# A fused state-space scan and squared-ReLU feed-forward: a new order for the front of the program

## The chip, the cores and the metric

One core of a Trainium2 chip runs the whole kernel. The metric is device time in microseconds, the median of several executions, lower being better. TensorE (PE in the profile, PEld for its weight loads), VectorE (DVE), ScalarE (ACT), GpSimd (POOL) and the DMA queues each work through a list of instructions of their own, in order, and wait for each other by semaphores. So the order in which the kernel records instructions decides what stands behind what on each engine.

## What is computed

Four batches of eight heads over 768 steps go through a chunked linear recurrence; its output, 3072 rows of 256, goes through a feed-forward layer with a squared ReLU. All inputs and the output are float32.

```python
for c in range(nc):                                   # chunks of 32 steps
    cum = np.cumsum(la, axis=-1)                      # la = log a
    L = np.exp(cum[..., :, None] - cum[..., None, :]) * causal
    M = np.einsum('bhin,bhjn->bhij', Cc, Bc) * L
    y_intra = np.einsum('bhij,bhjd->bhid', M, xc)
    y_inter = np.einsum('bhin,bhnd->bhid', Cc, state) * np.exp(cum)[..., None]
    y[:, :, sl] = y_intra + y_inter
    state = decay_full * state + np.sum(Bx, axis=2)   # Bx = B x decay_from_j
h = np.maximum(y_rows @ w_in, 0.0)                    # (3072,256) @ (256,2048)
out = h * h @ w_out                                   # (3072,2048) @ (2048,256)
```

## The kernel before

**Units and blocks.** The rows are cut into twelve units of 256 steps, one batch each: units 0 to 3 are the first third of the steps for the four batches, 4 to 7 the second, 8 to 11 the last. A unit's result, T, is one block of 256 rows of the feed-forward part; the blocks are called a to l.

**A unit, step by step.** `pc`, `pb` and `px` scale C, cast B and scale x by the running products of the decay, C and B into the tile jt, x into xs. `tr` transposes jt on TensorE (for the first four units) and `tc` copies the result out of PSUM into bct, in halves. `mt` computes the scores into PSUM banks 0 to 3, one bank for each quarter. Each quarter is multiplied by the causal mask: by VectorE straight out of PSUM (`mk`), or by a copy on ScalarE (`sc`) and then a product on VectorE or GpSimd (`ms`). `u` computes the state sums, `in` (or its halves `ina` and `inb`) applies the masked scores to the values, and `ca` adds what the earlier state carries in. `t` copies the two PSUM halves of the block into T (the letters behind the colon name the engine of each half), `us` copies the state sums. `sf` makes the state for the second half of a first-third unit (the tile Sd) directly from PSUM, `za`/`zb` and `sa`/`sb` the later ones.

**A block.** Up-projection `a0` to `a7`: four matmuls of 256 columns into one PSUM bank, two contraction halves for each of two output halves, then a ReLU on ScalarE (tile hb). `qa0` squares on VectorE (tile h). Down-projection `A0` to `A7`: four matmuls of 256 columns into an accumulator in bank 6 or 7. The same with the letters b to l. So T[a] and the w_in group are needed for an up-projection, a square and the w_out group for a down-projection.

**Decay products.** `sk` scans the first 256 steps, `sp` transforms the result on TensorE, `su` sums it, `to` and `ps` copy it out, `iv` takes inverses, `fq` spreads the totals into Pquad. `sn`, `p2` and `pq` are the same for the other 512 steps: `sn` ends with pick_p on VectorE, `p2` is eight transform matmuls and two of the totals.

**Loads.** The inputs of the units go through the SP queue (and a few through ACT's), in the order of the units. The weights, 2 MB each in float32, are cast on the way in by transfers that GpSimd issues (`wi0` to `wi3`, `wo0` to `wo3`, two up- or down-projections' worth each), so their place in GpSimd's own list of instructions sets when they start.

**Idle matmuls.** `id3:512` is three matmuls of ones with 512 columns whose result nobody reads, into a PSUM bank that is free.

**What sets the order.** `ORDER` is a text of such names, worked off from the first to the last by `one`; the tile framework adds the waits. A small bookkeeping (`turn`, `busy`, `bank`) hands out PSUM banks 0 to 5 in the order in which they were last used. From `rg4` on, the units 4 to 11 and the blocks c to l follow a regular rhythm.

Of the kernel before, what the change touches and what calls it, by code (L numbers as in the profile page):

```python
# [30 lines left out]
def kernel(  # L31
# [18 lines left out]
        ldx0:l:a wm jz0:v mb jz1:v ldB1:s id3:512 sk pbh0:a id2:512 pk pbl0:p wi0 sp pc0:v ldC1:s trB0 wi1 su iv1:0:8  # L50
        trC0 tcC0:0:v tcB0:2:a id1:512 tcC0:1:a ps pb1:a to px0:v jz2:v mt0 id1:512 u0:67 ldx1:s pc1:p fq sc0 mk0
        id1:512 mk0 ms0:p tr1 tc1:1:v sc0 tc1:0:a sf0 mt1 ldB2:s wo0 ldC2:s ms0:v ldx2:s id1:384 in0 ca0 iv:8:16
        id3:512 px1:p t0:aa id1:256 mk1 a0 a1 mk1 mk1 mk1 u1 ina1 inb1 sn1 us0 sf1 qa0 a3 ldC3:s wi2 fr p2 wi3 ca1
        qa1 wo1 pc2 pb2:a t1:vv us1 iv:32:64 a2 zb0 qa2 zb1 A0 ldB3:s wo2 ldx3:s b3 qb3 b0 pq b2 b1 tr2 wo3 sb1 qa3
        qb0 A1 b5 b4 qb1 qb2 qb5 tc2:1:v qb4 tc2:0:a a5 B0 b6 B1 a7 qa5 iv:16:32 px2 a6 mt2 B3 A2 sc2 u2 b7 us2 pb3:a
        pc3 mk2 qa6 px3 mk2 A5 ms2:v mk2 ld4 qb6 sf2 a4 qa7 B5 pc4 A6 A3 ld5 pb4 ina2 inb2 tr4 ca2 t2:aa tr3 B4 B2
        tc3:0:a tc3:1:a u3:45 qb7 ld6 ld7 mt3 qa4 B6 mk3 mk3 mk3 mk3 us3 c4 c5 c0 A4 A7 B7 c6 qc0 za3 qc4 c1 qc5 qc6
        sa3 px4 qc1 pc5 pb5 bk c2 rg4 tr5 C0 mk4 mk4 qc2 c7 qc7 sb0 c3 qc3 d2 d1 C5 za4 afC2 d0 C1 px5 C4 qd2 zb3 C6
        C3 qd0 d3 C2 mk4 mk4 C7 px6 sa4 rg5 qd3 sb3 pc6 zb4 sb4 pb6 D0 d4 qd1 tr6 mk5 za5 zb5 sa5 sb5 D1 iv:64:96 mk5
        d5 qd4 D2 pb7 d6 qd5 d7 qd6 D3 zb2 e0 qd7 mk5 e1 qe0 sb2 D4 mk5 D5 ld8 pc7 e2 qe1 D6 e3 qe2 px7 D7 rg6 e4 qe3  # L60
        za6 sa6 tr7 zb6 mk6 e5 qe4 sb6 e6 qe5 e7 qe6 mk6 E0 E1 E2 E3 ld9 px8 mk6 f0 qe7 E4 f1 qf0 pc8 E5 pb8 E6 mk6
        f2 qf1 f3 qf2 E7 rg7 mk7 F0 f4 qf3 za7 tr8 F1 F2 f5 qf4 f6 qf5 f7 qf6 g0 qf7 zb7 sa7 sb7 mk7 F3 mk7 F4 pc9
        pb9 px9 ld10 g1 qg0 F5 mk7 g2 qg1 F6 g3 qg2 F7 rg8 za8 zb8 sa8 sb8 g4 qg3 G0 mk8 tr9 g5 qg4 G1 mk8 g6 qg5 G2
        g7 qg6 G3 mk8 h0 qg7 G4 pc10 pb10 px10 ld11 h1 qh0 G5 mk8 h2 qh1 G6 h3 qh2 G7 rg9 za9 zb9 sa9 sb9 h4 qh3 H0
        mk9 tr10 h5 qh4 H1 mk9 h6 qh5 H2 h7 qh6 H3 mk9 i0 qh7 H4 pc11 pb11 px11 i1 qi0 H5 mk9 i2 qi1 H6 i3 qi2 H7
        rg10 za10 zb10 sa10 sb10 i4 qi3 I0 mk10 tr11 i5 qi4 I1 mk10 i6 qi5 I2 i7 qi6 I3 mk10 j0 qi7 I4 j1 qj0 I5 mk10
        j2 qj1 I6 j3 qj2 I7 rg11 za11 zb11 sa11 sb11 j4 qj3 J0 mk11 j5 qj4 J1 mk11 j6 qj5 J2 j7 qj6 J3 mk11 k0 qj7 J4
        k1 qk0 J5 mk11 k2 qk1 J6 k3 qk2 J7 rg12 k4 qk3 K0 k5 qk4 K1 k6 qk5 K2 k7 qk6 K3 l0 qk7 K4 l1 ql0 K5 l2 ql1 K6
        l3 ql2 K7 l4 ql3 L0 l5 ql4 L1 l6 ql5 L2 l7 ql6 L3 ql7"""
    WIN = [(0, 2), (2, 4), (4, 6), (6, 8)]  # L70
    WOUT = [(0, 2), (2, 4), (4, 6), (6, 8)]

# [154 lines left out]

    def ph_mask(k, q):
        nc.vector.tensor_tensor(out=live[k]["mts"][:, q].rearrange("p r g i -> p (r g i)"),  # L229
                                in0=pp[:, q, :], in1=mask, op=ALU.mult)  # L230
# [533 lines left out]
```

## Time and profile before

| | us |
|---|---|
| three runs of the kernel | 116.53, 116.64, 118.09 |
| their median | 116.64 |
| the profiled execution | 116.84 |
| its span, from the first instruction to the last | 115.1 |
| TensorE busy within the span | 108.9 (95%) |
| VectorE, ScalarE, GpSimd busy | 84.2, 76.7, 49.8 |

The granted clock of TensorE was 1.00 throughout. Times in a row of the timeline are the start from the beginning of the span and the length, both in microseconds; a row with x4 is four instructions merged, from the start of the first to the end of the last. What stands in square brackets is the engine's idle time just before the row, and what ended it. In the chain of waits a row is a stretch of time, with what the last instruction waited for at that point. TensorE's rows overlap by the depth of its pipeline, so that starts, not lengths, are compared. L numbers are lines of the kernel.

### The profile page before, as it was taken

How to read it: one execution, taken by the hardware profiler on the slowest of the kernel's cores; microseconds unless marked ns; L12 is line 12 of the kernel's file. 1: busy time of each engine (PE TensorE's matmuls, PEld its weight loads, DVE VectorE, ACT ScalarE, POOL GpSimd, SP SyncE). 2: the span in 40 equal slices, each digit the busy share in tenths (PEclk: the TensorE clock that was granted, in tenths of full speed). 3: DMA queues.
4: the chain of work that ended last, by engine and by line, in shares of the span. 5: the costliest groups of instructions: out<-in, count | busy, mean ns of one | idle time of the engine just before them, and what ended most of it. 6: DMA issues, size and time to landing. Idle time of an engine off the chain costs nothing.

```text
span 115.1 us, 3998 instructions
## 1 busy us (share of the span) xinstructions
PE 108.9 (95%) x1623; PEld 93.5 (81%) x1623; DVE 84.2 (73%) x187; ACT 76.7 (67%) x161; POOL 49.8 (43%) x102
## 2 busy tenths in 40 slices
PE   7977969999999999999999999999999999999990
PEld 2344749978898989989989989989989899899980
DVE  2469996779599969969965989849668488445530
ACT  0655667865598756787486686786777776876840
POOL 7369972068599457548602669038020020000000
PEclk9999999999999999999999999999999999999999
DMA  1999999989999913935915926623023020020202
GB/s 29 199 196 145 199 203 189 215 167 210 180 191 211 214 24 108 160 89 155 179 46 122 178 97 123 132 95 73 0 100 68 0 100 0 6 91 0 91 0 91
DMA packets 47814, 13.46 MB, mean 117 GB/s; under 512 B 44276, under 2 KB 45876, under 8 KB 47796
## 3 DMA queue, kind: packets, MB, share of 16 engines
q1 hardware_dynamic: 43828, 10.64, 44.8%
q0 software_dynamic: 1664, 2.10, 10.8%
q10 hardware_dynamic: 2304, 0.48, 2.0%
q8 instruction: 12, 0.20, 0.8%
q14 instruction: 6, 0.05, 0.1%
HBM read 10.58 MB, written 3.15 MB: 119 GB/s over the span
## 4 chain that ended last, share of the span: by engine, by line
PE 87%; DMA 6%; POOL 2%; issue 1%; DVE 1%; ACT 1%; ACTq 0%; DVEq 0%
PE pp L430 36%; PE pp L403 36%; PE pp L245 6%; DMA w_out_b<-in_moe_w_out_dram 6%; PE pp L476 4%; PE pp L220 3%; POOL mts L238 1%; PE pp L195 1%; POOL jt L158 1%; PE pp L452 1%; DVE jt L158 0%; DVE Sd L343 0%; ACT bct L208 0%; PE pp L521 0%; ACT osl L722 0%
## 5 line engine op out<-in xcount | busy, mean ns | idle before, releaser
L408 ACT ACTIVATE hb<-pp 128x512 bf16<-128x512 f32 x96 | 55.0, 599 | 24.7 <-PE pp L403 23.1
L430 PE MATMUL pp<-w_out_b,h 128*128 128x256 bf16 (+1 forms) x400 | 54.3, 268 | 0.8 <-DMA w_out_b<-in_moe_w_out_dram 0.8
L414 DVE TENSOR_TENSOR h<-hb 128x512 bf16<-128x512 bf16 x96 | 45.0, 486 | 12.7 <-ACT hb L408 12.3
L403 PE MATMUL pp<-T,w_in_b 128*128 128x256 bf16 x384 | 54.2, 273 | 0.0
L403 PEld LDWEIGHTS <-w_in_b 128*128 128x128 bf16 x384 | 41.4, 114 | 2.2 <-issue 1.0
L430 PEld LDWEIGHTS <-h 128*128 128x128 bf16 x400 | 37.6, 98 | 5.4 <-DVE T L210 1.1
L229 DVE TENSOR_TENSOR mts<-pp,mask 128x512 bf16<-128x512 f32 x45 | 29.6, 677 | 3.3 <-PE pp L220 3.3
L331 POOL TENSOR_TENSOR Sd<-z,Pquad 128x256 bf16<-128x256 f32 x16 | 11.1, 693 | 32.9 <-DVE z L315 25.7
L177 POOL TENSOR_TENSOR xs<-x_nat,Pinv 128x256 bf16<-128x256 f32 (+1 forms) x19 | 14.4, 776 | 5.2 <-DVE Pinv L546 4.6
L158 POOL TENSOR_TENSOR jt<-C_nat,P_sb 128x128 bf16<-128x128 f32 x22 | 9.4, 449 | 1.5 <-ACT P_sb L688 1.0
L476 PE MATMUL pp<-const-bfloat16-1.0 128*128 128x512 bf16 (+2 forms) x19 | 7.3, 516 | 0.8 <-PEq L748 0.8
L315 DVE SCALAR_TENSOR_TENSOR z<-z,Ptot,us 128x64 f32<-128x64 f32 x8 | 2.2, 281 | 6.3 <-ACT us L299 5.4
L437 ACT COPY osb<-pp 128x512 f32<-128x512 f32 x11 | 6.3, 584 | 0.4 <-PE pp L430 0.4
L245 PE MATMUL pp<-mts,xs 64*32 64x128 bf16 x384 | 5.9, 219 | 0.1
L170 POOL CAST jt<-B_nat 128x128 bf16<-128x128 f32 x17 | 5.4, 341 | 1.4 <-DMA B_nat<-in_B_dram 1.4
L220 PE MATMUL pp<-bct 32*64 32x256 bf16 x192 | 5.1, 279 | 0.9 <-DVE bct L210 0.6
L476 PEld LDWEIGHTS <-const-bfloat16-1.0 128*128 128x128 bf16 x19 | 2.2, 122 | 4.0 <-issue 3.7
L245 PEld LDWEIGHTS <-xs 64*32 64x32 bf16 x384 | 4.2, 90 | 0.6 <-issue 0.4
L282 ACT CAST T<-pp 128x512 bf16<-128x512 f32 x7 | 4.1, 592 | 0.4 <-PE pp L245 0.2
L208 ACT CAST T<-pp 128x256 bf16<-128x256 f32 x8 | 2.6, 375 | 2.6 <-PE pp L245 2.6
L245 PE MATMUL pp<-bct,Sd 128*128 128x128 bf16 x40 | 4.2, 220 | 0.0
L220 PEld LDWEIGHTS <-bct 32*64 32x64 bf16 x192 | 2.1, 102 | 2.0 <-issue 0.6
(62 smaller groups left out, 53.4 us busy)
## 6 DMA issues: line engine op xcount, KB each, us to landing
x_nat<-in_x_dram SPq DMA_DIRECT2D x11, 256.0 KB, 3.7
out_dram<-osb SPq DMA_DIRECT2D x11, 256.0 KB, 3.2
B_nat<-in_B_dram SPq DMA_DIRECT2D x11, 128.0 KB, 3.1
C_nat<-in_C_dram SPq DMA_DIRECT2D x11, 128.0 KB, 3.4
w_in_b<-in_moe_w_in_dram POOLq DMA_DIRECT2D x4, 256.0 KB, 6.8
w_out_b<-in_moe_w_out_dram POOLq DMA_DIRECT2D x4, 256.0 KB, 8.2
x_nat<-in_x_dram ACTq DMA_DIRECT2D x2, 128.0 KB, 3.4
bct<-jt SPq DMA_TRANSPOSE x8, 3.6
```

The source lines that it names most:

```text
L158: eng.tensor_tensor(out=_fap(jt[k % 3], 128 + 144 * g, [[384, 2], [32, 4], [1, 16]]), in0=_fap(loaded[k]["C"], 128 * g, [[16, 2], [32, 4], ...
L177: eng.tensor_tensor(out=_fap(xs, 256 * r, [[256, 2 // n], [32, 8], [1, 32]]), in0=_fap(loaded[k]["x"], 32 * r, [[32, 2 // n], [64, 8], [1, ...
L220: nc.tensor.matmul(pp[64 * u:64 * u + 64, q, r * 256:r * 256 + 256], bct[32 * q:32 * q + 32, r, 0, u * 64:u * 64 + 64], _fap(bct[32 * q:32 ...
L229: nc.vector.tensor_tensor(out=live[k]["mts"][:, q].rearrange("p r g i -> p (r g i)"), in0=pp[:, q, :], in1=mask, op=ALU.mult)
L245: nc.tensor.matmul(dst, w, v, start=bool(need), stop=False, skip_group_check=True, **({} if pos is None else {"tile_position": pos}))
L331: nc.gpsimd.tensor_tensor(out=_fap(S_d, 0, [[128, 2], [32, 4], [1, 32]]), in0=_fap(z, 0, [[32, 2], [0, 4], [1, 32]]), in1=_fap(Pquad, 4 * ...
L403: nc.tensor.matmul(pp[:, h, i * 256:(i + 1) * 256], _fap(w, g * w.shape[2] + (o // 2) * 512 + 2 * (o % 2) + i, [[4, 128]]), T[blk][:, g].r ...
L408: nc.scalar.activation(out=hb.rearrange("p i t -> p (i t)"), in_=pp[:, h, :], func=AF.Relu)
L414: nc.vector.tensor_tensor(out=h2, in0=hb, in1=hb, op=ALU.mult)
L430: nc.tensor.matmul(dst, h2[:, i, r * 128:(r + 1) * 128], w_out_b[gi][:, 2 * o + i, c0:c1], start=first, stop=(fp == 7 and i == 1), skip_gr ...
L437: nc.scalar.copy(out=osb, in_=pp[:, 6 if blk == 1 else 7, :])
L476: nc.tensor.matmul(pp[:, h, 0:int(cols)], ones_b[:, 0:128], ones_b[:, 0:int(cols)] if dep is None else dep, start=True, stop=True, skip_gr ...
```

## The change

The ORDER up to `rg4` is written anew, and from there on it is as before. The up-projection gets a form with a part, `a3:0` and `a3:1`, which issues the two matmuls of the first and then of the second contraction half; between the two the bank is held. `sf` gets a form on ScalarE (`sf2:a`), four activations that scale by a column of Pquad. Other new helpers (scores by halves, T by halves, named banks) are there but not called: `HALF` is empty, and no name with `@`, `tg` or `ca` with a part stands in the ORDER.

In the ORDER itself:

- Unit 0: one idle matmul of 256 columns is added ahead of `sp`. The inverses come ahead of C's product, the C transposes ahead of the totals `su`, and 1408 idle columns ahead of the C transposes. Three quarters are masked by VectorE out of PSUM and one by a copy and GpSimd, where it was two and two. Between `in0` and `ca0` stand 1024 idle columns; the 1792 behind `ca0` are gone.
- GpSimd: clearing jt2 (`jz2`) and the B casts of units 1 to 3 are GpSimd's now; they were VectorE's and ScalarE's. `wo0` stands ahead of `fq` and `ms0`.
- Copies: T0 is split between VectorE and ScalarE, T1 is ScalarE's; both copies of unit 1's transposes are ScalarE's.
- VectorE: `sf1` stands ahead of the second scan `sn`, and the scan behind unit 1's masks and the T0 copy; the products `px2` and `px4` are VectorE's (GpSimd's before).
- TensorE: a3, a2, b0, b2, b5, a7, a6 and b6 are up-projections in two parts. b0, b1 and half of b2 stand ahead of `A0`.
- Unit 2: its four quarters are masked by VectorE, `sf2` is ScalarE's. Unit 3: one quarter goes by ScalarE and GpSimd.

The core of the diff:

```diff
-        ldx0:l:a wm jz0:v mb jz1:v ldB1:s id3:512 sk pbh0:a id2:512 pk pbl0:p wi0 sp pc0:v ldC1:s trB0 wi1 su iv1:0:8
+        ldx0:l:a wm jz0:v mb jz1:v ldB1:s id3:512 sk pbh0:a id2:512 pk pbl0:p id1:256 sp trB0 id1:512 id1:384 iv1:0:8
...
-    def mm1(blk, fp):
-
-        h = bank()
+    opened = {}
+
+    def mm1(blk, fp, part=None):
+
+        h = opened.pop((blk, fp)) if part == 1 else bank()
         gi, o = group_of(WIN, fp)
         w = w_in_b[gi]
         for i in range(2):
-            for g in range(2):
+            for g in (0, 1) if part is None else (part,):
                 nc.tensor.matmul(pp[:, h, i * 256:(i + 1) * 256],
                                  _fap(w, g * w.shape[2] + (o // 2) * 512 + 2 * (o % 2) + i, [[4, 128]]),
                                  T[blk][:, g].rearrange("p r u t -> p (r u t)"),
-                                 start=(g == 0), stop=(g == 1), skip_group_check=True)
+                                 start=(g == 0 and (part is None or i == 0)), stop=(g == 1), skip_group_check=True)
+        if part == 0:
+            opened[(blk, fp)] = h
+            busy.add(h)
+            return
+        busy.discard(h)
...
-    def ph_sd_first(k):
+    def ph_sd_first(k, eng=None):
...
+        if eng is nc.scalar:
+            for q in range(4):
+                nc.scalar.activation(out=_fap(S_d, 32 * q, [[128, 2], [1, 32]]),
+                                     in_=_fap(pp, v["h"][0] * 512 + 256, [[32, 2], [1, 32]]),
+                                     func=AF.Copy, scale=Pquad[:, total(0, b, 0), q:q + 1])
+            v["S"] = [None, S_d]
+            return
```

On GpSimd, from the second w_in transfer on, there stood before (jt1 is unit 1's tile for B and C, sc0 a copied quarter of unit 0's scores and mts0 its masked scores):

```order
L139 DMA w_in_b1_113<-in_moe_w_in_dram 128x2x512
L158 TENSOR_TENSOR jt1_110<-C_nat1_179,P_sb_105 128x2x4x16 x2
L527 TENSOR_TENSOR Pquad_108<-Ptot_107,quad_93 128x32
L238 TENSOR_TENSOR mts0_218<-sc0_0_241,mask_90 128x512
L143 DMA w_out_b0_116<-in_moe_w_out_dram 128x1024
L177 TENSOR_TENSOR xs1_324<-x_nat1_236,Pinv_106 128x512
```

Unit 1's C product was the first thing behind the transfer. With the change, from the same transfer on:

```order
L142 DMA w_in_b1_113<-in_moe_w_in_dram 128x2x512
L749 MEMSET jt2_111 128x768
L173 CAST jt1_110<-B_nat1_159 128x2x4x16 x2
L161 TENSOR_TENSOR jt1_110<-C_nat1_193,P_sb_105 128x2x4x16 x2
L146 DMA w_out_b0_116<-in_moe_w_out_dram 128x1024
L572 TENSOR_TENSOR Pquad_108<-Ptot_107,quad_93 128x32
L257 TENSOR_TENSOR mts0_219<-sc0_2_232,mask_90 128x512
L180 TENSOR_TENSOR xs1_288<-x_nat1_222,Pinv_106 128x512
```

The clearing and two casts now stand ahead of the C product, and the first w_out transfer ahead of Pquad and the masked quarter.

On VectorE, around unit 1's masks and the second scan, there stood before (Sd is a state, a_cl, cp and pick_p the second scan, h a square):

```order
L343 TENSOR_TENSOR Sd0_0_258<-pp_120,Pquad_108 128x256
L238 TENSOR_TENSOR mts0_218<-sc0_3_255,mask_90 128x512
L546 RECIPROCAL Pinv_106<-P_sb_105 128x2x8
L229 TENSOR_TENSOR mts1_276<-pp_120,mask_90 128x512 x4
L468 TENSOR_SCALAR a_cl128_100<-a_nat128_98 128x128
L469 SCALAR_TENSOR_TENSOR cp128_102<-a_cl128_100,const-float32-0.0 128x128
L532 TENSOR_SCALAR pick_p128_104<-pick_94,cp128_102 128x16
L343 TENSOR_TENSOR Sd1_0_399<-pp_120,Pquad_108 128x256
L414 TENSOR_TENSOR h20_0_401<-hb0_0_335 128x512
```

The scan followed the four masks directly. With the change:

```order
L376 TENSOR_TENSOR Sd0_0_290<-pp_120,Pquad_108 128x256
L242 TENSOR_TENSOR mts1_285<-pp_120,mask_90 128x512
L213 CAST T0_330<-pp_120 128x4x64
L242 TENSOR_TENSOR mts1_285<-pp_120,mask_90 128x512 x3
L376 TENSOR_TENSOR Sd1_0_383<-pp_120,Pquad_108 128x256
L513 TENSOR_SCALAR a_cl128_100<-a_nat128_98 128x128
L514 SCALAR_TENSOR_TENSOR cp128_102<-a_cl128_100,const-float32-0.0 128x128
L577 TENSOR_SCALAR pick_p128_104<-pick_94,cp128_102 128x16
L459 TENSOR_TENSOR h20_0_408<-hb0_0_337 128x512
```

The T0 half stands behind the first mask of unit 1, and the state Sd1 ahead of the scan.

More of the change, by code (lines that the diff above doesn't have):

```diff
@@ L54 @@
[L54 to L63, printed above, removed]
```

98 lines of the change are left out of this document (76 added, 22 removed).

## The prediction

> **What bounds the kernel now.** I read the page first, then the chain of waits, then each engine's timeline up to 30 us. Page and chain:
>
> ```profile
> span 115.1 us, 3998 instructions
> PE 108.9 (95%) x1623; PEld 93.5 (81%) x1623; DVE 84.2 (73%) x187; ACT 76.7 (67%) x161; POOL 49.8 (43%) x102
> ```
>
> ```profile
> 10.33 6.49 DMA w_out_b<-in_moe_w_out_dram
> ...
> 27.48 0.42 DVE Sd L343
> ...
> 27.94 0.68 PE pp L245 x31
> ...
> 33.56 1.31 PE pp L403 x12
> ...
> 112.26 0.27 ACT osl L722
> ```
>
> TensorE is the bound. From 27.94 to the last copy at 112.26 the chain never leaves it, and the order behind rg4 is untouched. A 256-column matmul takes 1.31/12 = 0.109 us, so an up- or down-projection (four) takes 0.44. The change can only move the time at which this stream gets going. TensorE's own rows of the front:
>
> ```profile
> 0.85 4.85 PE L476 MATMUL pp<-const-bfloat16-1.0 128*128 128x512 bf16 x11 [0.85 <-PEq L748]
> ...
> 7.24 0.40 PE L195 MATMUL pp<-eye_b,jt 128*128 128x128 bf16 x4
> ...
> 10.94 0.45 PE L245 MATMUL pp<-mts,xs 64*32 64x128 bf16 x32
> 11.31 0.28 PE L245 MATMUL pp<-bct,Sd 128*128 128x128 bf16 x2
> 11.44 0.93 PE L476 MATMUL pp<-const-bfloat16-1.0 128*128 128x512 bf16 x4
> 12.20 1.03 PE L403 MATMUL pp<-T,w_in_b 128*128 128x256 bf16 x8
> ...
> 15.09 0.39 PE L537 MATMUL pp<-pick_p,spread 128*128 128x16 f32 x2 [0.27 <-DVE pick_p L532]
> 15.42 0.28 PE L245 MATMUL pp<-bct,Sd 128*128 128x128 bf16 x2
> ...
> 16.96 0.60 PE L430 MATMUL pp<-w_out_b,h 128*128 128x256 bf16 x4 [0.81 <-DMA w_out_b<-in_moe_w_out_dram]
> ...
> 26.35 1.47 PE L430 MATMUL pp<-w_out_b,h 128*128 128x256 bf16 x12
> ```
>
> Unit 0's block is applied to its values at 10.94 (in0), carried at 11.31 (ca0), copied to T, and the first up-projection starts at 12.20. Two stalls lie behind it. Before 16.96 the first down-projection, A0, waits 0.81 for w_out. At 27.94 unit 2's block (in2) waits for VectorE: twelve matmuls from 26.35 are through at 27.66, so it loses 0.28. These two, 1.1 us, are all that the edit could win there; the rest is what it does to the chain up to 12.20.
>
> **The change, part by part.** The rows that carry the terms, GpSimd first, then VectorE and ScalarE:
>
> ```profile
> 0.91 0.20 POOL L480 TENSOR_SCALAR_AFFINE_SELECT quad<-const-float32-1.0 128x4 f32<-128x4 f32 x1 [0.39 <-POOLq L748]
> ...
> 1.56 0.29 POOL L480 TENSOR_SCALAR_AFFINE_SELECT eye_b<-const-bfloat16-1.0 128x128 bf16<-128x128 bf16 x1
> ...
> 3.01 0.10 POOL L134 MEMSET B_nat<- 128x1 f32 x1
> ...
> 5.61 1.64 POOL L139 DMA_DIRECT2D w_in_b<-in_moe_w_in_dram  x2 [0.17 <-issue]
> ...
> 8.24 0.82 POOL L158 TENSOR_TENSOR jt<-C_nat,P_sb 128x128 bf16<-128x128 f32 x2 [1.00 <-ACT P_sb L688]
> 9.04 0.23 POOL L527 TENSOR_TENSOR Pquad<-Ptot,quad 128x32 f32<-128x32 f32 x1
> 9.24 1.15 POOL L238 TENSOR_TENSOR mts<-sc,mask 128x512 bf16<-128x512 bf16 x1
> ...
> 14.22 0.78 POOL L158 TENSOR_TENSOR jt<-C_nat,P_sb 128x128 bf16<-128x128 f32 x2
> ...
> 16.14 0.59 POOL L143 DMA_DIRECT2D w_out_b<-in_moe_w_out_dram  x1
> ...
> 28.12 0.92 POOL L170 CAST jt<-B_nat 128x128 bf16<-128x128 f32 x2
> ...
> 32.90 0.73 POOL L170 CAST jt<-B_nat 128x128 bf16<-128x128 f32 x2
> ```
>
> ```profile
> 4.68 0.22 DVE L468 TENSOR_SCALAR a_cl<-a_nat 64x128 f32<-64x128 f32 x1 [0.99 <-DMA a_nat<-in_a_dram]
> ...
> 11.00 2.42 DVE L229 TENSOR_TENSOR mts<-pp,mask 128x512 bf16<-128x512 f32 x4
> ...
> 13.34 0.37 DVE L468 TENSOR_SCALAR a_cl<-a_nat 128x128 f32<-128x128 f32 x1
> ...
> 14.20 0.84 DVE L532 TENSOR_SCALAR pick_p<-pick,cp 128x16 f32<-128x16 f32 x1
> ...
> 14.96 0.41 DVE L343 TENSOR_TENSOR Sd<-pp,Pquad 128x256 bf16<-128x256 f32 x1
> ...
> 15.96 0.74 DVE L210 CAST T<-pp 128x256 bf16<-128x256 f32 x2
> ```
>
> ```profile
> 5.67 0.30 ACT L512 ACTIVATE pick_p<-pick,cp 64x8 f32<-64x8 f32 x1
> ...
> 29.04 0.88 ACT L208 COPY bct<-pp 128x384 bf16<-128x384 bf16 x2
> ```
>
> *Up to unit 0's scores: +0.05.* An idle matmul of 256 columns is added ahead of the first transforms (L452): half of 4.85/11, 0.22. VectorE now takes the inverse before C's product, but the C transposes no longer stand behind the totals (L521). They come out at 7.3 against 7.24. The 1408 idle columns put ahead of them take 0.6 at the rate of the four idle rows (1792 columns in 12.20 − 11.44 = 0.76), and run while the transposes would wait anyway.
>
> *GpSimd's queue: +0.5 on in0.* After the two w_in issues end (5.61 + 1.64 = 7.25) GpSimd now clears jt2 (moved from VectorE) and casts unit 1's B (moved from ScalarE) before C's product; then come w_out, Pquad and the mask product ms0, which stood ahead of w_out before. A memset of 768 elements is in no row. Bounds: 0.10 (one element) and 1.7 (the two-input product over 512 elements, 1.15, times 1.5); less than nothing it can't be, as it stands in a queue that in0 waits for. The affine selects give the slope of a one-input operation: 0.09 for 124 elements more, hence 0.20 + 0.56; since clearing reads nothing I take 0.7. The pair of casts costs 0.73 to 0.92 at 28 to 33 us; I take 0.7. Then: 7.25 + 0.7 + 0.7 + 0.82 = 9.45 for C's product (before 9.06), 0.6 for w_out, 0.2 for Pquad, 1.15 for ms0: 11.4. in0 needs ms0, so it goes from 10.94 to 11.45. [...]
>
> The scores of unit 1 (mt1) come no later than that: its transposes start at 9.5 and take 0.35, both copies follow on ScalarE in 0.88, the scores at 10.8.
>
> *ca0 to the first up-projection: +0.25 more.* Behind in0 (0.37, as from 10.94 to 11.31) stand 1024 idle columns, 0.43, then ca0. Idle matmuls after ca0 are gone. T0 is copied by VectorE and ScalarE at once: one of them 0.41 instead of two on ScalarE. in0 11.45, idle 11.82, ca0 12.25, T0 done 12.9, a0 at 12.95 against 12.20: together +0.75.
>
> *VectorE up to the second totals: the gate.* In its queue T0's half stands behind the first of unit 1's masks, ahead of the other three, the state Sd1 and the scan: 12.9 + three masks of 0.605 = 14.7, Sd1 0.36, a_cl and scan 0.8: pick_p starts at 15.9. It took 0.84 for 16 elements, against 0.22 for the 128 of the first a_cl; it ends at 15.04 where GpSimd's product (14.22 + 0.78) ends at 15.00, so most of it was waiting. GpSimd's queue has at 15.9 its casts of unit 2 (product at 14.4, w_out issue, casts 15.8 to 16.45): between 0.2 and 0.84, I take 0.5. That is 16.4. [...] TensorE meanwhile has 2.9 us to do between 12.95 and 16.4 (six and a half projections and the small blocks) and waits, so the totals (L537) run at 16.45 and the next matmul starts 0.33 later (15.42 − 15.09): 16.78.
>
> *The wait for w_out: −0.18 net.* Before, everything up to the second totals, a3 and a2 was done when A0 started at 16.96. Now the same is done at 16.78, and ten matmuls of the second block (b0, b1, half of b2) come ahead of A0: 1.09, so A0 is at 17.9. w_out is issued at 9.4 in place of 10.33; with the 6.49 of the chain it lands by 16, and even the old 16.82 would do. So the wait of 0.81 goes, but the later front eats 0.63 of it. An idle matmul of 128 columns behind A0 costs 0.05.
>
> *Halves.* Up-projections cut by contraction half have the same four matmuls; each half still reads both copies of T. They cost nothing and start nothing earlier by themselves.
>
> *Unit 2: −0.28.* Sd2 moves to ScalarE: four ACTIVATEs at 0.30 (the row that also scales by a column), 1.2 at most, against 0.41 on VectorE. It starts when unit 2's sums are out at about 25 and is needed behind six projections (2.6 us): 1.4 to spare. VectorE then has four masks and a square, 2.8, from 24.8: 27.6, when TensorE reaches in2. xs2's product is VectorE's now, and unit 3's B cast is GpSimd's, where it waits for B; behind it are queued the unit's C and x products, of which C's waited for a transfer before too:
>
> ```profile
> 24.82 0.84 POOL L158 TENSOR_TENSOR jt<-C_nat,P_sb 128x128 bf16<-128x128 f32 x2 [0.46 <-DMA C_nat<-in_C_dram]
> ```
>
> ```profile
> 20.00:24.00 4.00, 4.00 (x51) 3.51 (x50) 2.47 (x7) 3.44 (x8) 0.69 (x1) 1.00 1.21 215
> ```
>
> The second row, of the busy time by stretch, gives of 4 us TensorE 4.00, weight loads 3.51, VectorE 2.47, ScalarE 3.44, GpSimd 0.69: there is room for both. If that cover is gone, the 0.28 stays.
>
> *w_in and w_out behind it.*
>
> ```profile
> w_out_b<-in_moe_w_out_dram POOLq DMA_DIRECT2D x4, 256.0 KB, 8.2
> ```
>
> By the sums above the middle ones are issued within 0.3 of before. The last w_out, behind the second Pquad in both orders, moves with the totals: 16.14 + (16.45 − 15.09) = 17.5. With the median of 8.2 it lands at 25.7, and its first reader, A6, now stands behind unit 2's block at 28.
>
> Sum: −0.18 + 0.05 − 0.28 = −0.4, of which the choices of 0.7, 0.7 and 0.5 may give or take 0.5. I put −0.3. The profiled execution took 116.84 (115.1 of span, 1.7 around it), 0.2 over the median of the runs, 116.64. So 116.54 against 116.84, and **116.35 as a median**.
>
> **Rivals.** *GpSimd's queue is the new bound (slower).* For: in0 hangs on the end of a GpSimd queue with a memset and two casts more in it. Against: the casts alone have short rows. Decision point: memset and casts together above 1.7 (1.4 taken, plus the 0.3 won); from there each 0.1 more is 0.1 on the end. At 1.7 + 0.92 it ends 1.2 − 0.3 = 0.9 slower: 117.5.
>
> *The front is quicker than I have it.* Memset 0.3, casts 0.6, and pick_p meets no GpSimd instruction (0.2): 0.45 + 0.3 earlier, 115.6. Against: masks and scores of unit 1 hold in0 at 11.0 anyway.
>
> *The clock of TensorE.* Idle matmuls ran at 0.44 per 512 columns up to 5.6, and at 0.22 from 11.44: it doubled in between. If it doubles later, the 1408 columns take 1.2, the scores of unit 0 come 0.55 later, and what GpSimd's queue does not cover of that, 0.3, is lost: 116.65. [...]
>
> *Unit 2's wait stays*, because masks and px2 are late: 0.28 to 0.6 back, 116.7 to 117.0.
>
> **How the numbers follow.** Forecast 0.48 (115.95 to 116.75), GpSimd slower 0.22, quicker front 0.13, clock 0.05, unit 2 0.05, something in the second block that I don't see 0.07, of which most would be a stall above 2 us. Range: 115.5 lies just under the quick case, 117.4 just inside the slow one's end; what is left out is the unseen stall and the ends of the two, under 2 in 10. 2% (2.3 us) is about what a measurement of this kernel can tell from no change. No case reaches a gain of that size, since the stalls sum to 1.1: 0.02. Slower by that much needs the unseen stall: 0.06. Within: 0.92.
>
> **What would show it.** Right: in0 at 11.3 to 11.6, released by GpSimd; a0 near 12.9; no DMA wait at A0; the second totals released by pick_p near 16.5; no VectorE step in the chain at 28. Wrong: in0 at 11.0 (memset cheap), or past 11.8; a wait of TensorE above 0.3 us between 18 and 36; L403 or L430 matmuls at another rate.

## The result and the profile after

| | before | changed |
|---|---|---|
| median of 20 runs, us | 116.56 | 117.81 |
| fastest, slowest, us | 115.69, 123.53 | 116.88, 119.79 |
| the profiled execution, us | 116.84 | 117.42 |
| its span, us | 115.1 | 115.4 |
| runs with a mean granted clock of 0.986 or less | 48 of 122, in the later sessions | 0 of 32, with the 12 of e4 below |

The ratio is 1.0111, 95% interval 1.0082 to 1.014: the change made the kernel slower, by 1.1%, which is inside the 2% that the prediction called no change; the forecast was 116.35, and the time lies above the end of its range, 117.4. The ratio leaves out runs more than 1.5% above the fastest, 37 of the 48 in the last row among them, in which TensorE's clock fell, and of these two kernels only the one before had such runs.

The page of the changed kernel begins so (span and instructions, then busy time, share and count of each engine):

```profile
span 115.4 us, 4013 instructions
PE 109.9 (95%) x1630; PEld 94.4 (82%) x1632; DVE 85.1 (74%) x186; ACT 76.5 (66%) x159; POOL 51.8 (45%) x107
```

TensorE is the bound as before. Its timeline, and under it GpSimd's, VectorE's and ScalarE's, at the places that the prediction names (start, length, engine, line, what; in brackets the idle time ahead of a row):

```profile
5.84 0.64 PE L497 MATMUL pp<-eye_f,cp 64*64 64x32 f32 x8
...
6.53 0.98 PE L521 MATMUL pp<-const-bfloat16-1.0 128*128 128x512 bf16 x4
7.35 0.38 PE L198 MATMUL pp<-eye_b,jt 128*128 128x128 bf16 x4
...
11.45 0.60 PE L264 MATMUL pp<-mts,xs 64*32 64x128 bf16 x32
...
12.44 0.27 PE L264 MATMUL pp<-bct,Sd 128*128 128x128 bf16 x2
13.17 1.03 PE L443 MATMUL pp<-T,w_in_b 128*128 128x256 bf16 x8 [0.46 <-ACT T L211]
...
16.83 0.40 PE L582 MATMUL pp<-pick_p,spread 128*128 128x16 f32 x2
...
18.16 0.60 PE L475 MATMUL pp<-w_out_b,h 128*128 128x256 bf16 x4
...
27.92 0.62 PE L264 MATMUL pp<-mts,xs 64*32 64x128 bf16 x32
...
28.82 1.04 PE L475 MATMUL pp<-w_out_b,h 128*128 128x256 bf16 x8
...
35.42 0.42 PE L223 MATMUL pp<-bct 32*64 32x256 bf16 x16
36.06 0.60 PE L475 MATMUL pp<-w_out_b,h 128*128 128x256 bf16 x4 [0.21 <-ACT osb L482]
```

```profile
7.44 0.76 POOL L749 MEMSET jt<- 128x768 bf16 x1
8.12 0.81 POOL L173 CAST jt<-B_nat 128x128 bf16<-128x128 f32 x2
8.91 0.76 POOL L161 TENSOR_TENSOR jt<-C_nat,P_sb 128x128 bf16<-128x128 f32 x2
...
10.44 1.15 POOL L257 TENSOR_TENSOR mts<-sc,mask 128x512 bf16<-128x512 bf16 x1
```

```profile
15.96 0.28 DVE L577 TENSOR_SCALAR pick_p<-pick,cp 128x16 f32<-128x16 f32 x1
...
26.82 1.27 DVE L242 TENSOR_TENSOR mts<-pp,mask 128x512 bf16<-128x512 f32 x2
```

```profile
35.41 0.59 ACT L482 COPY osb<-pp 128x512 f32<-128x512 f32 x1
```

Three things are to be seen. The first up-projection, a0, starts at 13.17, behind ScalarE's half of the T copy; before it was 12.20. The wait of A0 for w_out is gone (no bracket at 18.16), and no wait stands at unit 2's block (27.92). But at 36.06 there is a bracket that the trace of before has not: block c's first down-projection, C0, waits for ScalarE. Before, the same place read:

```profile
35.42 0.42 PE L220 MATMUL pp<-bct 32*64 32x256 bf16 x16
35.77 0.61 PE L430 MATMUL pp<-w_out_b,h 128*128 128x256 bf16 x4
```

```profile
33.16 1.08 ACT L437 COPY osb<-pp 128x512 f32<-128x512 f32 x2 [0.17 <-PE pp L430]
```

C0 needs the accumulator bank that block a held. In the new order a's last down-projection, A7, stands behind c2, so the copy that frees the bank (osb) runs at 35.41, behind a ReLU; before, both copies were through at 34.24. Unit 4's scores, the row ahead of C0, start at 35.42 in both profiles: up to there the two are level, and the 0.29 by which C0 is later, nearly all of the 0.3 between the spans, comes at this one place.

The inputs land at a different time in each profile (unit 0's B cast, which waits for its load, starts at 5.07 before, 5.27 after, 4.99 in e4 and 5.26 in e5), so the experiments below count from unit 0's first transforms (5.63 before, 5.84 after): a0 at 6.57 and 7.33, A0 at 11.33 and 12.32 (with ten matmuls, 1.09, now ahead of it), C0 at 30.14 and 30.22. For this first pair the count hides 0.21 of the change: in both profiles the transforms start without a wait as the idle matmuls ahead of them end, and the added 256 columns make these 0.21 longer. All that the removed waits gave, the front and C0 took back.

### The profile page after: what moved, and what is told of

The parts are those of the page before. It is cut to its first block, busy times and chain, and to the rows that moved or that the text cites. A ratio compares the mean times of both kernels' runs of the same rounds, so it can differ in the third digit from the quotient of the medians.

```text
span 115.4 us, 4013 instructions
## 1 busy us (share of the span) xinstructions
PE 109.9 (95%) x1630; PEld 94.4 (82%) x1632; DVE 85.1 (74%) x186; ACT 76.5 (66%) x159; POOL 51.8 (45%) x107
## 4 chain that ended last, share of the span: by engine, by line
PE 87%; POOL 4%; DMA 3%; ACT 2%; issue 1%; ACTq 1%; DVE 0%; POOLq 0%
PE pp L443 37%; PE pp L475 37%; PE pp L264 7%; PE pp L223 3%; DMA B_nat<-in_B_dram 3%; POOL w_in_b L142 1%; PE pp L521 1%; POOL jt L173 1%; PE pp L198 1%; POOL jt L161 1%; ACT hb L453 1%; POOL jt L749 0%; ACT osb L482 0%; ACT bct L211 0%; ACTq L128 0%
## 5 line engine op out<-in xcount | busy, mean ns | idle before, releaser
L242 DVE TENSOR_TENSOR mts<-pp,mask 128x512 bf16<-128x512 f32 x46 | 30.3, 678 | 2.9 <-PE pp L223 2.9
L180 POOL TENSOR_TENSOR xs<-x_nat,Pinv 128x256 bf16<-128x256 f32 (+1 forms) x16 | 12.6, 806 | 0.0
L173 POOL CAST jt<-B_nat 128x128 bf16<-128x128 f32 x23 | 7.0, 331 | 8.5 <-PE pp L264 6.8
L521 PE MATMUL pp<-const-bfloat16-1.0 128*128 128x512 bf16 (+3 forms) x26 | 8.4, 439 | 1.5 <-PEq L813 0.8
L521 PEld LDWEIGHTS <-const-bfloat16-1.0 128*128 128x128 bf16 x28 | 2.9, 116 | 4.8 <-issue 4.3
L264 PE MATMUL pp<-mts,xs 64*32 64x128 bf16 x384 | 6.4, 219 | 0.1
L211 ACT COPY bct<-pp 128x384 bf16<-128x384 bf16 (+1 forms) x6 | 2.6, 443 | 2.0 <-PE pp L198 2.0
```

The source lines that it names most:

```text
L173: eng.tensor_copy(out=o, in_=i)
L180: eng.tensor_tensor(out=_fap(xs, 256 * r, [[256, 2 // n], [32, 8], [1, 32]]), in0=_fap(loaded[k]["x"], 32 * r, [[32, 2 // n], [64, 8], [1, ...
L264: nc.tensor.matmul(dst, w, v, start=bool(need), stop=False, skip_group_check=True, **({} if pos is None else {"tile_position": pos}))
L521: nc.tensor.matmul(pp[:, h, 0:int(cols)], ones_b[:, 0:128], ones_b[:, 0:int(cols)] if dep is None else dep, start=True, stop=True, skip_gr ...
```

## The experiments

Names such as e3 are those of the runs. All times in this table are from runs on a chip beside the kernel before; "high clock" are the runs with a mean granted clock above 0.986.

| | kernel | median | ratio, 95% interval | clock low | median, high clock | minus before's, same session |
|---|---|---|---|---|---|---|
| | before, four sessions | 116.98, 116.91, 117.04, 116.85 | | 48 of 122 | 116.71, 116.41, 116.65, 116.40 | |
| e1 | new front, old rest | 117.61 | 1.0019 (0.9974 to 1.0065) | 3 of 12 | 117.27 | +0.56 |
| e2 | old front, new rest | 118.28 | 0.9951 (0.9897 to 1.0006) | 8 of 12 | 116.41 | −0.30 |
| e3 | changed, output of a early | 117.31 | 1.0026 (0.9985 to 1.0067) | 2 of 12 | 117.11 | +0.40 |
| e4 | changed, again | 117.31 | 1.0064 (1.003 to 1.0099) | 0 of 12 | 117.31 | +0.60 |
| e5 | before, again | 116.92 | 1.0026 (0.9984 to 1.0068) | 3 of 10 | 116.62 | +0.21 |
| e6 | changed, GpSimd relieved | 117.16 | 1.0071 (1.003 to 1.0112) | 0 of 12 | 117.16 | +0.75 |
| e7 | e2, output of a early | 117.03 | 1.0017 (0.9973 to 1.006) | 3 of 12 | 116.51 | +0.10 |
| e8 | e6, output of a early | 117.03 | 1.0028 (0.9991 to 1.0066) | 0 of 12 | 117.03 | +0.62 |
| e9 | before, idle columns | 117.02 | 1.0024 (0.9985 to 1.0063) | 1 of 12 | 116.83 | +0.18 |
| e10 | changed, fewer idle columns | 119.32 | 1.021 (1.014 to 1.028) | 5 of 6 | 118.82 | +2.17 |
| e11 | e7, transposes first | 116.37 | 1.0006 (0.9965 to 1.0046) | 4 of 12 | 116.36 | −0.29 |
| e12 | e11, idle columns | 116.69 | 1.0009 (0.9969 to 1.0049) | 0 of 12 | 116.69 | +0.04 |
| e13 | e3, transposes first | 116.92 | 1.0032 (0.9995 to 1.007) | 1 of 12 | 116.89 | +0.49 |
| e14 | e8, transposes first | 116.29 | 1.0002 (0.9966 to 1.0038) | 0 of 12 | 116.29 | −0.11 |

The first session of four kernels (e1 to e4) has the first of before's medians, e5 to e8 the second, e9 to e12 the third, e13 and e14 the last. The kernel before moves by 0.3 from session to session, so kernels of different sessions are compared by the last column. The kernel before itself, as e5, has +0.21 there: differences under 0.25 are not read. By the ratio only e4, e6 and e10 have an interval that leaves out 1, so the smaller steps below rest on the last column alone.

### Front and rest apart (e1, e2)

The two orders were joined where unit 1's state sums are copied. e1 is the changed order up to `p2`, and then the old one:

```diff
-p2 wo2 pb2:p b0:0 ldB3:s pq zb1 qa2 b1 ldx3:s b2:0 qa1 b0:1 wo3 iv:32:64 A0 ...
+p2 wo2 pb2:p qa1 iv:32:64 zb0 qa2 zb1 A0 ldB3:s ldx3:s b3 qb3 b0 pq b2 b1 tr2 wo3 sb1 ...
```

> The changed order up to the second totals (p2), then the old order from A0 on, without the parts already done. Theory 1 (the new front starts TensorE's stream later, and what the wait for w_out used to swallow now reaches the end): about 0.8 to 1.2 us slower than before, 117.4 to 117.8. Theory 2 (the rest costs it: block a's output copy held back, unit 2's masks and state): within 0.4 of before, 116.4 to 117.0, and C0 does not wait for a copy of the output.

e2 is the old order up to `a2`, and then the changed one:

```diff
-a2 zb0 qa2 zb1 A0 ldB3:s wo2 ldx3:s b3 qb3 b0 pq b2 b1 ...
+a2 wo2 b0:0 ldB3:s pq zb0 zb1 qa2 b1 ldx3:s b2:0 b0:1 wo3 A0 qb0 ld4 b3 qb1 ...
```

> The old order up to a2, then the changed order from the second block's up-projections on. Theory 1: only the 0.3 of the wait at C0 is left, 116.6 to 117.0. Theory 2: most of the loss is here, 117.4 to 117.9. Both: C0 waits 0.2 to 0.3 for block a's output copy on ScalarE, as in the changed kernel's profile.

At high clock e1 had 117.27 and e2 116.41, where the changed kernel had 117.31 and the kernel before 116.71. That points to the new front, but does not prove it: e2's figure is of four runs, and e1's ratio, 1.0019, has 1 well inside its interval. Neither came out as a theory had it: e1's +0.56 lies between the two, e2's 116.41 below both. In e1, whose profiled execution was a long one (118.76), A0 waits 0.75 for w_out again, although its transfer was issued at 9.58 (10.33 before): the earlier issue did not make it land earlier there (A0 started 8.35 after it, in place of 6.63). In e2 A0 doesn't wait, as it stands behind ten more matmuls; but these now wait themselves, for the copy of unit 1's T, which VectorE makes in the old front:

```profile
16.15 1.33 PE L442 MATMUL pp<-T,w_in_b 128*128 128x256 bf16 x10 [0.72 <-DVE T L212]
```

So in the old front the stall ahead of A0 was not there to be won as a whole: of the 0.81, 0.72 came back under another name. C0 waits 0.22 for the same copy as in the changed kernel. And 8 of e2's 12 runs were at 118.1 to 118.9 with a mean clock of 0.985 or 0.971, which no theory had.

### Block a's output early (e3, e4)

```diff
-... B6 B7 mk3 ms3:p c0 ld7 mk3 ... za3 px4:v A4 qc4 ... pb5 A7 qc1 ...
+... B6 B7 mk3 A4 A7 ms3:p c0 ld7 mk3 ... za3 px4:v qc4 ... pb5 qc1 ...
```

> The changed kernel with A4 and A7, the last down-projections of block a, moved up behind B7, so that ScalarE copies block a's output before block c needs the accumulator. Theory 1: the wait of 0.21 before C0 goes and the span is 0.3 shorter than the changed kernel's; 0.3 of the 1.25 comes back, 117.4 to 117.6. Theory 2: 0.6 or more comes back, 117.2 or less.

e4 is the changed kernel once more, for a second profile and a time on the same chip.

> The changed kernel once more, for a second profile. Theory 1: where its first loads land later than at 4.87 (a) or 5.25 (B), in0, the second totals and the end all come later by the same, as nothing behind them waits for a DMA; where they land alike, the span is 115.4 within 0.1. Theory 2: the front is as in the first profile and the spread comes from behind 18 us.

With A4 and A7 early the wait at C0 is gone (C0 at 35.70, no bracket). The high-clock median falls by 0.20, from 117.31 to 117.11, the size of the wait, but no more than the scatter. In e4's profile the front came 0.4 earlier than in the first profile, since its inputs landed earlier (the B cast of unit 0 at 4.99 in place of 5.27) and the 12 idle matmuls ahead of the transforms took 4.01 in place of 5.07. Yet the last matmul ended at 112.68, where it was 112.45, for another wait came up:

```profile
43.21 0.42 PE L223 MATMUL pp<-bct 32*64 32x256 bf16 x16 [0.36 <-DMA bct<-jt]
```

Unit 5's scores wait for the DMA that transposes its B and C (tr5). In SP's queue it stands behind unit 7's loads and block a's last store. Before:

```profile
36.50 2.11 SPq L186 DMA_TRANSPOSE bct<-jt  x1
```

In the changed kernel's first profile, and then in e4's:

```profile
37.06 1.45 SPq L483 DMA_DIRECT2D out_dram<-osb  x1
38.61 1.25 SPq L189 DMA_TRANSPOSE bct<-jt  x1
```

```profile
36.68 2.36 SPq L128 DMA_DIRECT2D x_nat<-in_x_dram  x1
39.14 0.53 SPq L483 DMA_DIRECT2D out_dram<-osb  x1
39.77 1.26 SPq L189 DMA_TRANSPOSE bct<-jt  x1
```

The transposes are issued 2.1 and 3.3 later than before. They land 3.3 to 3.7 after the issue, and unit 5's scores follow at about 43 (42.72 before): the new order had used up a slack of over 2 us that no wait in the trace of before shows. So the spread came from behind 18 us, as the second theory of e4 had it. Only part of it was this wait, though: e4's span is 0.7 longer than the first profile's, and 0.47 of that lies behind the last matmul, where the last store of the output took 2.2 to land in place of 1.7.

### The kernel before, once more (e5)

> The kernel before, unchanged, for a second profile. Theory (the wait for w_out is no fixed price): A0 waits anything from 0 to 0.8 us for w_out, by when the transfer lands, and the median stays within 0.4 of 116.6. Rival (the wait is fixed): A0 waits 0.7 to 0.9 again, and the stall was there to be won. In both, the first up-projection starts 6.5 to 6.7 us after unit 0's first transform.

A0 waited 0.69, just short of the rival's 0.7, so that this run alone does not tell the two apart. The row names VectorE's copy of T (done at 17.43), but w_out was issued at 10.45, and the shortest of its four transfers took 7.0, so that it landed then at the earliest, too. With 0.81 in the first profile, 0.43 in e9 and 0.75 in e1 the wait is there in each profile in which A0 stands at its old place, and its size differs. What neither theory had is that a0 came 7.41 after the first transforms, at 12.95, not at 12.20. TensorE's first rows in e5:

```profile
0.85 3.84 PE L476 MATMUL pp<-const-bfloat16-1.0 128*128 128x512 bf16 x11 [0.85 <-PEq L748]
5.54 0.43 PE L452 MATMUL pp<-eye_f,cp 64*64 64x32 f32 x8 [0.84 <-DVE cp L469]
...
6.64 0.36 PE L521 MATMUL pp<-pick_p,spread 64*128 64x8 f32 x2 [0.45 <-ACT bct L208]
```

The busy time of e5 by stretches of half a microsecond (stretch; length and TensorE's busy time; weight loads, VectorE, ScalarE, GpSimd; granted clock; DMA share and GB/s):

```profile
6.00:6.50 0.50, 0.18 (x2) 0.01 (x1) 0.48 (x2) 0.36 (x2) 0.50 (x1) 1.00 1.21 190
6.50:7.00 0.50, 0.36 (x3) 0.37 (x4) 0.00 (x0) 0.09 (x1) 0.50 (x2) 0.93 1.11 180
7.00:7.50 0.50, 0.50 (x5) 0.37 (x5) 0.40 (x2) 0.00 (x0) 0.43 (x1) 0.50 0.62 131
...
9.50:10.00 0.50, 0.50 (x4) 0.24 (x3) 0.50 (x1) 0.26 (x1) 0.50 (x1) 0.50 1.18 167
10.00:10.50 0.50, 0.50 (x6) 0.34 (x4) 0.01 (x1) 0.18 (x1) 0.50 (x2) 0.66 0.95 123
10.50:11.00 0.50, 0.04 (x1) 0.10 (x1) 0.35 (x2) 0.30 (x1) 0.50 (x2) 1.00 0.93 130
```

The mean of 0.93 makes the clock half for the last 0.07 of its stretch, the 0.66 for the first 0.34: it was at half from 6.93 to 10.34, 3.4 us. Ahead of that TensorE had waited twice, 0.84 for the first transforms and 0.45 for what follows them. The opening of the first two profiles ran at half the rate, too, which the granted clock does not show: the 11 idle matmuls took 4.85 in the kernel before, 0.44 each (in the changed kernel 5.07 for 11 and a half), where later ones take 0.22 (0.76 for 1792 columns from 11.44), so the 1.00 throughout holds only behind them. Here they took 3.84, so by these two rates about the last 1 us of them ran at the full one, an estimate, and both waits lie between that and the fall. Half the clock for 3.4 of 115.9 us is the mean of 0.985 that this run lists, and two such stretches make 0.971, the other value that comes up again and again. In the 3.4 us ahead of the fall, 3.52 to 6.93, TensorE was busy for 2.1, and ahead of the fall in e10 (4.79 to 8.20) for 2.5. No run shows the mechanism; whether the waits have a part in it, e9 and e10 try.

### GpSimd's queue relieved (e6, e8)

```diff
-... pb1:p mk0 ... px0:v jz2:p mt0 ...
+... pb1:a mk0 ... px0:v jz2:v mt0 ...
```

jt2 is cleared by VectorE again, and unit 1's B cast by ScalarE. e8 has A4 and A7 early as well.

> The changed kernel with two of its moves undone: clearing jt2 is VectorE's again, unit 1's B cast ScalarE's. Theory (GpSimd's queue ahead of ms0 makes the front late): in0 and a0 come 0.4 to 0.8 us earlier after unit 0's first transform (a0 at 6.6 to 6.95 after it, where the changed kernel has 7.33), and the median is 0.3 to 0.6 below the changed kernel's. Rival (VectorE's order and the scan set the second totals, whatever a0 does): a0 earlier or not, the totals stay within 0.2 of 3.7 us after a0, and the time within 0.2 of the changed kernel's. Rival (the idle columns hold TensorE): a0 moves by less than 0.2.

> The changed kernel with GpSimd's queue relieved as in the second run and A4, A7 early. Theory: both corrections add up, 0.6 to 1.0 below the changed kernel's median, so 0.2 below to 0.2 above before's. Rival (the front's loss is in VectorE's order, not in GpSimd's queue): only the 0.3 to 0.45 of the early output.

Counted from the first transforms, a0 came at 7.11 in e6 and 6.70 in e8 (7.33 in the changed kernel, 6.57 in that of before), so most of the late front was GpSimd's queue; in e6 the C product waited for its transfer and took 1.20 in place of 0.76. The second totals came 3.66 and 3.65 after a0, as in the changed kernel (3.66), which is what the first rival of e6 had. And the time did not follow: against before e6 stands at +0.75 and e8 at +0.62, where the changed kernel has +0.60 (e4) and e3 +0.40. The expected gains, 0.3 to 0.6 and 0.6 to 1.0, did not come. In e6's profile the wait at C0 grew to 0.46 and unit 5's transposes cost 0.24: what the front gave was lost there. (That execution took 118.84, one of its longest, but 1.5 of this lie behind the last matmul: its last store took 3.2 to land.) In e8's profile nothing waits from 14 us on, and its span was 114.3, but its median was no better, so most of its runs must lose time that this profile does not show.

### Transposes first (e7, e11, e13, e14)

e7 is e2 with A4 and A7 early.

> The order of before up to a2, the changed order from there on, with block a's last two down-projections (A4, A7) ahead of unit 3's masked copy. Theory (late front and late output of a are the two losses, and they add up): A0 starts as early as with the old front, block c's first down-projection waits for no copy, and the median of undisturbed runs is 0.4 to 0.9 below before's, 115.8 to 116.2. Rival (something behind the front gives it back): mt5 is no earlier than before's relative to the first transform, and the time is within 0.2 of before's.

The rival held: C0's wait was gone, A0 waited for nothing, and the time was no better than e2's (+0.10 against −0.30, of four runs). The profile shows where it went. The matmuls ahead of A0 wait 0.47 for unit 1's T, a down-projection at 28.31 waits 0.29 for a square, and then:

```profile
42.91 0.42 PE L222 MATMUL pp<-bct 32*64 32x256 bf16 x16 [0.59 <-DMA bct<-jt]
```

e11, e13 and e14 take e7, e3 and e8 and put unit 7's loads behind unit 5's transposes:

```diff
-... c0 ld7 mk3 ... rg4 tr5 C0 ...
+... c0 mk3 ... rg4 tr5 ld7 C0 ...
```

> The order of before up to a2, the changed rest, block a's output early as in the run before of that kind, and the loads of unit 7 behind the DMA transposes of unit 5 in SP's queue. Theory (the wait of 0.59 for unit 5's transposes is the load of unit 7 ahead of them): no wait of TensorE for a DMA near 43 us, transposes issued before 37.5, and the runs at full clock 0.3 to 0.6 below those of the run before of that kind (116.5), so 115.9 to 116.2 and 0.3 to 0.7 below before's. Rival (the transposes wait for GpSimd's B cast and C product, done at 35.5): issued past 38 as before, no gain.

> The changed kernel with block a's output early and unit 7's loads behind unit 5's transposes; its front is left as it is. Theory (the loss is late front, late output and late transposes): no wait of TensorE between 14 and 50 us, runs at full clock 0.3 to 0.6 below the changed kernel's 117.3, so 116.7 to 117.0, still 0.2 to 0.4 above before's, since the front is still late; no low runs. Rival (the new order costs somewhere else): above 117.1.

> As the run before, with jt2's clearing back on VectorE and unit 1's B cast back on ScalarE. Theory: a0 at most 6.9 after unit 0's first transform, runs at full clock 116.3 to 116.7, level with before's at full clock, and the median of all runs 0.1 to 0.5 below before's, since the granted clock does not fall. Rival: above 116.9, and something else of the new order costs.

In e14 SP's queue now reads

```profile
32.31 1.67 SPq L483 DMA_DIRECT2D out_dram<-osb  x2
34.85 1.33 SPq L189 DMA_TRANSPOSE bct<-jt  x1
36.23 1.38 SPq L128 DMA_DIRECT2D C_nat<-in_C_dram  x1
```

and no row of TensorE behind 13 us has a wait. In e11 the transposes went at 36.35, and its one wait behind the front is 0.61 for unit 1's T, at 17.26. The high-clock medians are 116.36 (e11), 116.89 (e13) and 116.29 (e14). e11 fell short of its theory, 115.9 to 116.2; e13 and e14 came out within 0.1 of theirs, but for one run of e13 with a low clock. These two ran in one session and differ by GpSimd's two moves alone: 0.60, where the same two moves were worth nothing with the transposes late (e4 to e6, +0.60 to +0.75; e3 to e8, +0.40 to +0.62). Moving unit 7's loads gave 0.39 in the old front (e7 to e11, +0.10 to −0.29) and 0.73 in the relieved one (e8 to e14), and nothing with the late front (e3 to e13), where TensorE itself comes later. These steps are smaller by the ratio, 0.30% from e13 to e14 and 0.26% from e8 to e14, with intervals that overlap. That the transposes come too late in most runs of e8, and TensorE late enough for them in most of e3, is an inference, as one profile of each doesn't show it.

### Idle columns (e9, e10, e12)

e9 puts the idle matmuls of the new front into the kernel before, e12 puts them into e11, and e10 takes them out of the changed kernel:

```diff
 e9, e12
-... ldC1:s trB0 wi1 su ...
+... ldC1:s trB0 id1:512 id1:384 id2:512 wi1 su ...
 e10
-... pbl0:p id1:256 sp trB0 id1:512 id1:384 iv1:0:8 id2:512 pc0:v trC0 ...
+... pbl0:p sp trB0 iv1:0:8 pc0:v trC0 ...
```

> The kernel before with 1920 idle columns of TensorE (512, 384, 512, 512) ahead of unit 0's C transposes, where it otherwise waits. Theory (a gap of TensorE near 6 us lets its granted clock fall to half for about 3.4 us in a share of the runs, and the idle columns prevent it): runs whose mean granted clock is 0.985 or below fall from 27 of 70 to at most 1 of 12, the median falls by 0.2 to 0.5 below before's, and the undisturbed runs are 0 to 0.2 slower. Rival (the idle columns only cost): low runs stay at 3 to 6 of 12, the median rises by 0.1 to 0.3.

> The changed kernel without the 256 idle columns ahead of the first transforms and without the 1920 ahead of the C transposes. Theory: low runs (mean granted clock 0.985 or below), of which the changed kernel had none in 32, come up in 3 to 6 of 12, and the runs at full clock are 0 to 0.3 faster than the changed kernel's 117.3. Rival (the idle columns are what makes the changed kernel slower): no low runs, and 0.4 to 0.8 faster.

> The kernel before this with the 1920 idle columns ahead of unit 0's C transposes. Theory (both causes are right and independent): no low runs, the median of all runs 0.6 to 1.0 below before's, the best of all kernels here. Rival (old front and idle columns conflict): full-clock runs 0.3 or more above the kernel before this.

Runs with a low clock went from 13 of 29 (before, same session) to 1 of 12 in e9 and none in e12, and to 5 of 6 in e10. There, the page's row of granted clocks (40 slices of the span, in tenths) and a0:

```profile
PEclk9985558999999999999999999999999999999999
```

```profile
14.48 1.87 PE L443 MATMUL pp<-T,w_in_b 128*128 128x256 bf16 x8 [0.46 <-ACT T L211]
```

a0 came 8.65 after the first transforms (14.48 − 5.83), 1.3 later than with the idle columns, and the first two up-projections took 1.87 in place of 1.03. So the idle columns mostly keep the clock up. They do not always: over all sessions the clock was low in 7 of 128 runs of the kernels that have them (3 of 12 in e1, which has the same front) and in 71 of 174 of those that do not. Without them the changed kernel took 119.32 in place of 117.31, but not all of these 2 us are such falls: the one run of e10 without one took 118.82, where the theory had 117.0 to 117.3, and why stays open. And the idle columns have a price where the clock would have held: e9's high-clock median is 116.83 against 116.65 (within the scatter), e12's 116.69 against e11's 116.36, as the rival of e12 had it. The median of all runs therefore gained nothing in e9 (117.02 against 117.04) and 0.35 in e12 (116.69), where the theories had 0.2 to 0.5 and 0.6 to 1.0.

Part of that price is not in the profiled span at all. A run's time less its span is 1.65 to 2.00 in the 122 runs of the kernel before. It is above 2.1, up to 2.8, in 18 of the 128 runs of the kernels with the new idle columns, and in none of the 52 of e2, e5, e7, e10 and e11, which lack them. e12 and e11 differ by 0.33 in time, but only by 0.05 in the median of their spans at high clock (114.75 and 114.70). No run shows what happens outside the span.

## Why the prediction was wrong

The forecast was 1.46 too low (116.35 for 117.81). Three steps failed that the timeline shows: VectorE's scan was not the gate of the second totals, TensorE's own work was; the net for the wait of w_out was therefore mis-sized, +0.11 in place of −0.18; and the release of block a's accumulator was in no term, and cost 0.29 at C0. Together with about half of unit 2's wait they make the 0.70 by which C0 came later than forecast. The rest, about as much again, is in no profile, as the end of this section says.

**Up to unit 0's scores: +0.05.** Right: they came at 8.20, 0.11 later than before. The count of idle columns ahead of the C transposes was wrong, though: the row at 6.53 is four matmuls, 512 + 384 + 512 + 512 = 1920, not 1408. They hold the C transposes until 7.35.

**GpSimd's queue: +0.5 on in0.** Right in each term: memset 0.76 for 0.7, casts 0.81 for 0.7, in0 at 11.45 for 11.45. But ms0 ended at 11.59, not at 11.4, so in0 took 0.60 in place of 0.45 while it waited for its last quarter.

**ca0 to the first up-projection: +0.25 more.** Mis-sized: ca0 came at 12.44 for 12.25, and a0 at 13.17 for 12.95. Together +0.97 for +0.75.

**VectorE up to the second totals: the gate.** This step failed. pick_p was done at 16.24, near the 16.4 of the sum, and released nothing; it took 0.28. The totals came at 16.83 because TensorE got there no earlier: from a0 it worked 3.66 us without a listed wait, where the sum gave it 2.9 (it has four projections ahead of the totals, not six and a half). The 2.9 was the old distance, 12.20 to 15.09; the new order puts a2, ca1 and 512 idle columns ahead of the totals as well. In the seven other profiles of this front with its clock up (e1, e3, e4, e6, e8, e13, e14) the totals come 3.65 to 3.79 after a0, and pick_p was done 0.2 to 0.9 earlier.

**The wait for w_out: −0.18 net.** The mechanism was right, A0 at 18.16 without a wait; the late front ate more than was allowed for: 16.96 and the 1.09 of the ten matmuls make 18.05, so the net was +0.11 in place of −0.18. That the wait could be won held in this front, where ScalarE copies unit 1's T; in the old front most of it came back as the wait for that T (0.72 in e2, 0.47 in e7, 0.61 in e11).

**Halves.** Nothing spoke against their costing nothing: up- and down-projections run at 0.109 us a matmul as before (17.07 to 18.16 for ten).

**Unit 2: −0.28.** No wait is listed any more, but from in2 to the next down-projection it took 0.90 (27.92 to 28.82), where e14 has 0.74 (27.08 to 27.82). The masks ended at 28.09, not at 27.6, so 0.16 of the 0.28 stayed, inside the block instead of ahead of it.

**What the prediction did not have** is block a's output. I followed the moved projections for what they need, and not for what they free. A7 late means its copy late and C0 late, and the transposes of unit 5 late in SP's queue. The sum had C0 0.41 earlier than before, at 35.36; it came at 36.06. Of these 0.70, 0.29 is C0's wait with its run-up (35.42 to 36.06 in place of 35.77), and 0.41 was gone by 35.42: 0.29 by the front (−0.18 to +0.11) and 0.16 by unit 2, which is 0.04 too much. The transposes cost nothing in the first profile, 0.36 in e4's. With the late front, the late output and the late transposes taken away together, in e14, the changed kernel is at 116.29, level with the kernel before in the same session, 116.40 (ratio 1.0002, 0.9966 to 1.0038). So together they are the loss that the later sessions show at high clock, +0.60 in e4. How it splits is clear for GpSimd's moves alone, 0.60 between e13 and e14.

**The rivals.** "GpSimd's queue is the new bound" came nearest in time, but not by its decision point: memset and casts took 1.57, less than 1.7, so that its 117.5 came near the 117.81 by luck. The quicker front fell with a0 at 13.17, and unit 2's wait stayed by half, as said. **The clock of TensorE** was a rival with the sign turned round. I let the new idle columns suffer from a late clock; in fact they mostly protect it (low in 7 of 128 runs with them), and it is the kernel before that loses its clock, in 48 of 122 runs. That is why the medians of all runs differ less (117.31 for e4 against 116.98 in its session) than the high-clock ones (117.31 against 116.71).

**What stays open.** The profiled execution of the changed kernel was 0.88 above the forecast for it (117.42 for 116.54): 0.6 in the span, which is the 0.70 above (the sum's −0.41 went into the forecast as −0.3), and 0.3 outside it (2.0 in place of 1.7). The median of its 20 runs lay another 0.39 higher, where the forecast had it 0.2 lower. The next 12 runs, in another session, had 117.31, again all at high clock. The late transposes may give such a spread, and with them early the times of e14 lay close (12 runs, 116.05 to 117.40), but the profiles do not show it. In the three long ones of this front, e1, e4 and e6, the last matmul is 3.8, 3.4 and 4.5 ahead of the end, where it is 2.9 to 3.0 in all the others, and the last store takes 2.5, 2.2 and 3.2 to land, in place of 1.7. The order of that place was not touched, and no run shows why the store is late there.

**A version that beats both?** By the ratio none does: e14 has 1.0002 and e11 1.0006, with 1 inside their intervals. By the median of all runs, e14 with 116.29 is 0.56 below the kernel before in its session (116.85) and e11 with 116.37 is 0.67 below (117.04 in its own), e14 because its clock did not fall in any run.

## What to carry to other kernels

When work is moved in a hand-written order, follow not only what each moved step needs but what its end frees: a bank, a copy behind it, a store, and whatever stands behind that store in its queue. Slack that shows no wait in the trace is still a price, so ask of each transfer how much earlier than needed it came. Gates in series hide each other: relieving GpSimd's queue was worth nothing here while the transposes came late, and 0.60 once they did not; and one execution's profile doesn't show how often a clock falls (1.00 in the first profile of the kernel before, low in 48 of its 122 runs), so the list of granted clocks of all runs is read with it.

## What was unexpected of the hardware

- TensorE's granted clock went back to 0.50 for 3.4 us in the middle of the front, behind waits of 0.84 and 0.45 us (e5), on a single core; a mean clock that fits one or more such falls came in 48 of 122 runs of one kernel and in none of 32 of the other. Four idle matmuls of 0.8 us in all took it from 13 of 29 runs to 1 of 12 (before and e9).
- Small operations of VectorE took longer beside a two-input product of GpSimd in some profiles, and not beside a cast in the two cases below. In e4 the a_cl of 128 elements took 1.07 beside C's product on GpSimd, in e14 0.22 without one; pick_p, 0.84 beside such a product in the kernel before (and again in e5), took 0.28 in the changed kernel in the middle of a GpSimd cast, and 0.23 in e4 (16.14, with the cast from 15.96 to 16.52):

```profile
14.57 1.07 DVE L513 TENSOR_SCALAR a_cl<-a_nat 128x128 f32<-128x128 f32 x1
```

```profile
14.64 0.78 POOL L161 TENSOR_TENSOR jt<-C_nat,P_sb 128x128 bf16<-128x128 f32 x2
```

```profile
15.90 0.54 POOL L173 CAST jt<-B_nat 128x128 bf16<-128x128 f32 x2
```

  The first ends at 15.64, after the product's 15.42, though its row starts 0.07 ahead of it, and the 0.84 began 0.02 ahead of its product (14.20 and 14.22) and ended 0.04 behind it (15.04 and 15.00); so by these rows the one that started first was not the first to be done. Nor does it happen each time: in e14 pick_p was done in 0.46, at 15.32, beside a product from 14.88 to 15.90, and in e13 it took 0.27 in the middle of a product. No run shows the mechanism.
- A w_out transfer issued 0.75 earlier (e1) landed no earlier: A0, waiting for it in both, started 8.35 after the issue, in place of 6.63 (16.96 − 10.33), in one profile of each.
